# Half of wq's last rows in lanes 0 to 63, and another order of the last group's products

## The chip, the cores and the metric

The kernel runs on one core of a Trainium2 chip. The metric is the device time of one execution in microseconds, the median of three runs. The profile is of one execution of the same program, taken by the hardware profiler.

## The reference

Two branches of a decoder block act on one token of each of four batch rows, and are added to the input. x has the shape 4 x 1 x 640; all data are bfloat16.

```
xn  = layernorm(x)
q   = xn @ wq                          # 640 x 4096: 32 heads of 128
s   = q . k_cache / sqrt(128)          # k_cache: 4 x 32 x 4096 x 128
o   = softmax(s) @ v_cache             # v_cache: the same shape
z   = gelu(xn @ w_in);  z1, z2 = halves of z;  z2 = layernorm(z2)
g   = w_sp * z2 + b_sp
out = x + o @ wo + (z1 * g) @ w_out
```

Each of the two caches is 134 MB, and every element is read once.

## The kernel before, in words

**Tiles.** The caches are read in 32 tiles each. A tile is one group of four heads (hg) of one batch row (b), 4 MB: 128 lanes of 32 KB. There are eight groups of four batch rows, taken in that order. `load` (L115) issues a tile on SP's queue into one of five buffers (`slot`, L79) of 32 KB a lane. `pump` (L137) issues the next load as soon as the buffer's former occupant has been used; the order is written out in `loads` (L125 to L132): two key tiles, then value and key in turn, with two extra key tiles late in the run. The last value tile goes in four pieces, cut by V_CUTS at 64, 96 and 112 of the 128 rows that a lane holds.

**Start.** ACT issues x (L83) and two single numbers, wsp and bsp (L94, L95). SP issues wq in two transfers (L89): five rows of wq belong to each lane, four of them (4096 KB) go into one buffer and the fifth (1024 KB, 8 KB a lane) into a second one. Then SP issues w_in and w_out in three transfers into a third buffer (L100 to L104), then the first key tiles. DVE and ACT normalise x, and PE transposes it (L202) into xnT, 128 lanes by five columns of four. q comes from 40 products (L217): for each half r of the eight groups and each of the five rows c, four products write four quarters of the PSUM lanes. Then follow `stage_q` (L379), which spreads q over the lanes, and `gmlp` (L268), the second branch.

**The loop** (L569) handles key tile i and value tile j = i minus the lag. DVE multiplies the key tile with q (`product`) and halves it (`fold_half`), PE sums it (`sums`), DVE and ACT make the softmax weights (`row_sums`, `head_max`, `exps`), and PE multiplies them into the value tile (`weighted`, L462): 32 products with the weights as the stationary operand and 512 value columns moving. Two batch rows (a = 0 or 1) of a group share one PSUM tile, `pvs[hg, a]`; `take` (L481) copies it to `o_rows` with ACT. The rows of a group stand spread in it, and products with a 0/1 matrix, `pick`, gather them (`group_pick`, L498); `group_proj` (L527) multiplies with a tile of wo into the sum that is kept in PSUM.

**The end** (L596 to L643) is written out by hand. `load_wo(7)` issues the last wo tile in four pieces of 160 KB, one for each head, behind the last value tile. Then, in PE's order: value tile 30 (32 products of L471), the sums of the weights (`den`, L604), the first 64 rows of value tile 31 as 16 wide products of L471, ACT's copy (`take`), 8 products with `pick` for both a (L616, each two instructions as the data are float32), and the remaining 64 rows of tile 31 as 64 narrow products (L625) in which the values are the stationary operand and four columns of weights move. DVE divides (L633), `group_proj` makes eight products (L531), and ACT and DVE copy the result out.

Inside the block of L563 the order on PE, DVE, ACT and SP is that of the program. Ahead of it the framework orders the instructions, and it places all semaphores by itself, those of the DMAs too.

Of the kernel before, what the change touches and what calls it, by code (L numbers as in the profile page):

```python
# [9 lines left out]
FP32 = mybir.dt.float32  # L10
BF16 = mybir.dt.bfloat16
# [10 lines left out]
def kernel(  # L22
# [14 lines left out]
    nc = tc.nc  # L37
    P = nc.NUM_PARTITIONS
    Bsz, Sq, D = A_x.shape
    _, H, S, Dh = A_k_cache.shape  # L40
    HD = A_wq.shape[1]
    F = B_w_in.shape[1]
    Fh = F // 2
    DC = D // P
# [4 lines left out]
    HT = 4  # L49
    HG = H // HT  # L50
    NT = HG * Bsz
    LN = P // HT
    NC = HT * S // P
# [8 lines left out]
    QD = 32  # L62
    CB = 4
    NG = NC // CB
    GW = CB * Dh
    MC = CB * HT

    const = ctx.enter_context(tc.tile_pool(name="const", bufs=1))
# [3 lines left out]
    small = ctx.enter_context(tc.tile_pool(name="small", bufs=2))  # L72
# [3 lines left out]
    ps_m = ctx.enter_context(tc.tile_pool(name="ps_m", bufs=3, space=PSUM))  # L76
    ps_out = ctx.enter_context(tc.tile_pool(name="ps_out", bufs=1, space=PSUM))

    def slot(name):  # L79
        return kv.tile([P, SLOT], BF16, tag="kv", name=name)  # L80
# [2 lines left out]
    nc.scalar.dma_start(out=x_bf[:], in_=A_x.flatten_outer_dims())  # L83

    wq_v = A_wq.rearrange("(p c) n -> p c n", c=DC)
    wq_parts = []
    for c0, c1 in ((0, HT), (HT, DC)):
        t = slot("wq")[:, 0 : (c1 - c0) * HD].rearrange("p (c n) -> p c n", n=HD)
        nc.sync.dma_start(out=t, in_=wq_v[:, c0:c1, :])  # L89
        wq_parts += [(t, i) for i in range(c1 - c0)]  # L90

    wsp_bf = const.tile([1, 1], BF16)
    bsp_bf = const.tile([1, 1], BF16)
# [8 lines left out]
        out=w_out_sb[:, 0:NFF, :], in_=B_w_out[0 : NFF * P].rearrange("(p k) n -> p k n", k=NFF)  # L102
# [10 lines left out]
    V_CUTS = (0, 64, 96, 112, NC)  # L113
# [45 lines left out]
    ident = const.tile([P, P], BF16)  # L159
# [5 lines left out]
    ones_sq = const.tile([P, P], FP32)  # L165
    nc.vector.memset(ones_sq[:], 1.0)

    NACC = 2
    p_m = [const.tile([P, NG, QD], BF16, name=f"pm{b}") for b in range(Bsz)]
    acc = [const.tile([P, HT, QD], FP32, name=f"acc{g}") for g in range(NACC)]  # L170
# [9 lines left out]
    for i in range(NSTAT):  # L180
# [5 lines left out]
        out=rstd[:], in_=mv[:, 1:2], func=ACT.Sqrt, bias=eps_tile[:Bsz], scale=1.0  # L186
    )
    nc.vector.reciprocal(out=rstd[:], in_=rstd[:])
    xn_bf = work.tile([Bsz, D], BF16)
    nc.vector.tensor_scalar(  # L190
        out=xn_bf[:],
# [9 lines left out]
    for c in range(DC):  # L201
        nc.tensor.transpose(  # L202
            out=xnT_ps[:, c, :], in_=xn_v[:, c, :], identity=ident[:Bsz, :Bsz]
        )
    xnT = const.tile([P, DC, QD], BF16)
    nc.vector.memset(xnT[:], 0.0)
    nc.vector.tensor_copy(out=xnT[:, :, 0:Bsz], in_=xnT_ps[:])

    QB = HG // CB
    q_rows = []  # L210
    for r in range(QB):
        q_ps = ps_pv.tile([P, GW], FP32, tag="pv", name="q_ps")
        for c in range(DC):
            t, i = wq_parts[c]
            for g in range(CB):
                hg = r * CB + g
                nc.tensor.matmul(  # L217
                    out=q_ps[g * QD : (g + 1) * QD, :],
                    lhsT=xnT[:, c, :],
                    rhs=t[:, i, hg * GW : (hg + 1) * GW],  # L220
                    start=(c == 0),
                    stop=(c == DC - 1),
                )
        rows = const.tile([P, GW], BF16, name=f"q_rows{r}")
        nc.vector.tensor_copy(out=rows[:], in_=q_ps[:])  # L225
        q_rows.append(rows)
# [5 lines left out]
        out=hot[:],  # L232
        in_=ident[:].rearrange("p (g t m) -> p t m g", g=P // QD, t=2),
# [3 lines left out]
    for a in range(2):  # L237
        for t in range(2):
            nc.vector.tensor_copy(
                out=pick[:, a, :, :, 2 * a + t],  # L240
                in_=hot[:, t, :].rearrange("p (c h) -> p c h", c=CB),
# [5 lines left out]
    def out_sum(half):  # L247
        return out_ps[OG * half : OG * half + Bsz, :]

    for half in range(2):  # L250
        nc.tensor.matmul(
            out=out_sum(half),
            lhsT=ident[:Bsz, :Bsz],
            rhs=x_bf[:, half * NOH : (half + 1) * NOH],
            start=True,
            stop=False,
# [122 lines left out]
    def stage_q(i):  # L379
        hg, b = divmod(i, Bsz)  # L380
        r, g = divmod(hg, CB)
        row = g * QD + b
        qb_ps = ps_m.tile([P, HT, Dh], FP32, tag="m", name="qbc_ps")
        nc.tensor.matmul(  # L384
            out=qb_ps[:],
            lhsT=ident[:, row : row + 1].to_broadcast([P, P]),
            rhs=q_rows[r][:],
            start=True,
            stop=True,
        )  # L390
        qbcs[i] = small.tile([P, Dh], BF16, name="qbc", bufs=3)
        for hh in range(HT):
            ps = slice(hh * LN, (hh + 1) * LN)
            nc.scalar.copy(out=qbcs[i][ps, :], in_=qb_ps[ps, hh, :])  # L394
# [64 lines left out]
                accum_out=a[ps, hh, b : b + 1],  # L459
            )  # L460

    def weighted(i, c1=NC):  # L462
        hg, b = divmod(i, Bsz)
        a, t = divmod(b, 2)
        if t == 0:
            pvs[hg, a] = ps_pv.tile([P, GW], FP32, tag="pv", name="pv")
        v_nat, pm = v_tiles[i], p_m[b]
        ng = c1 // CB
        for g in range(ng):
            cg = g % CB  # L470
            nc.tensor.matmul(  # L471
                out=pvs[hg, a][cg * QD : (cg + 1) * QD, :],
                lhsT=pm[:, g, :],
                rhs=v_nat[:, g * CB : (g + 1) * CB, :],
                start=(t == 0 and g < CB),
                stop=(t == 1 and g >= ng - CB),
            )

    gr, taken = {}, {}
# [1 line left out]
    def take(hg, a):  # L481
        o = taken[hg, a] = small.tile([P, CB, Dh], FP32, name="o_rows")
        nc.scalar.copy(out=o[:].rearrange("p c d -> p (c d)"), in_=pvs.pop((hg, a))[:])  # L483
# [59 lines left out]
    def at(i, fn, *args):  # L543
        if 0 <= i < NT:
            fn(i, *args)
# [17 lines left out]
    with tc.manual_schedule(engines={E.PE, E.DVE, E.Activation, E.SP}):  # L563
        stage_q(0)
        stage_q(1)
        gmlp()
        used.update(occupants[:3])
        pump()
        for i in range(NT):  # L569
            j = turns.get(i)  # L570
            last = turns.get(i - 1, -1)
            product(i, 0)
            at(i - 1, row_sums, 1)
            at(i - 1, head_max)
            group(last, group_pick)
            fold_half(i, 0)
            at(i - 1, exps)
            sums(i, 0)
            group(last, group_turn)
            if i + 2 < NT:  # L580
                stage_q(i + 2)
            product(i, 1)
            due = [] if j is None else [j]
            if i == NT - 1:
                due += range(j + 1, NT - 2)
            for jj in due:
                consume(jj)
            row_sums(i, 0)
            fold_half(i, 1)
            sums(i, 1)  # L590
            group(last, group_proj)
            used.add(("k", i))
            pump()
            if i % Bsz == 2 and i // Bsz < HG - 1:
                load_wo(i // Bsz)
        load_wo(HG - 1)  # L596
        row_sums(NT - 1, 1)
        head_max(NT - 1)
        exps(NT - 1)
        weighted(NT - 2)  # L600

        hg, b = HG - 1, Bsz - 1
        den = ps_m.tile([P, HT, Bsz], FP32, tag="m", name="den_all")
        nc.tensor.matmul(  # L604
            out=den[:], lhsT=ones_sq[:], rhs=acc[hg % NACC][:, :, 0:Bsz], start=True, stop=True
        )
        rden = small.tile([P, HT, Bsz], FP32, name="rden_all")
        nc.vector.reciprocal(out=rden[:], in_=den[:])  # L608

        weighted(NT - 1, V_CUTS[1])  # L610
        take(hg, 1)
        o_ps = ps_m.tile([P, HT, Bsz], FP32, tag="m", name="o_last")
        for a in range(2):
            o = taken.pop((hg, a))
            for c in range(CB):
                nc.tensor.matmul(  # L616
                    out=o_ps[:],
                    lhsT=o[:, c, :],
                    rhs=pick[:, a, c, :, 0:Bsz],
                    start=(a == 0 and c == 0),  # L620
                    stop=False,
                )
        pm = p_m[b][:].rearrange("p g (t c h) -> p g t c h", t=2, c=CB)
        for c in range(V_CUTS[1], NC):
            nc.tensor.matmul(  # L625
                out=o_ps[:, :, b],
                lhsT=v_tiles[NT - 1][:, c, :],
                rhs=pm[:, c // CB, b % 2, c % CB, :],
                start=False,
                stop=(c == NC - 1),  # L630
            )
        o_n = small.tile([P, HT, Bsz], BF16, name="o_n_last")
        nc.vector.tensor_tensor(out=o_n[:], in0=o_ps[:], in1=rden[:], op=ALU.mult)  # L633
        gr[hg] = o_n
        group_proj(hg)

        res = work.tile([P, NOH], BF16, name="res")
        out_v = out.flatten_outer_dims()
        r0, r1 = slice(0, Bsz), slice(OG, OG + Bsz)
        nc.scalar.copy(out=res[r0], in_=out_ps[r0])  # L640
        nc.vector.tensor_copy(out=res[r1], in_=out_ps[r1])
        nc.scalar.dma_start(out=out_v[:, 0:NOH], in_=res[r0])
        nc.sync.dma_start(out=out_v[:, NOH:D], in_=res[r1])  # L643
# [30 lines left out]
```

## Time and profile before

| What | Value |
|---|---|
| median of three runs | 666.87 us (666.75 to 668.23) |
| the profiled execution: its own time | 668.35 us |
| the profiled execution: span from first to last instruction | 666.6 us |
| busy: PE, DVE, ACT | 46%, 75%, 19% of the span |
| bytes read, mean rate | 282.24 MB, 423 GB/s |
| rate in the first and the last of 40 slices | 373 and 243 GB/s |
| rate in the slices between | 421 to 439 GB/s |
| mean TensorE clock granted | 0.734 of full speed |

The page gives, for each engine, the busy time; the span cut into 40 slices; the DMA queues; the chain of work that ended last, followed back from the last instruction; and the costliest groups of instructions. A busy share is a mean over stages with different limits. In a timeline row stand start, duration, engine, line, operation, the tile written and the tiles read, the count, and in brackets the idle time before it with what ended it. SPq and ACTq rows are issues of DMAs: their duration is that of the issue and not of the transfer, and a row that holds two issues covers the wait between them. A tile's view gives the time from a DMA's issue to its landing.

### The profile page before, as it was taken

How to read it: one execution, taken by the hardware profiler on the slowest of the kernel's cores; microseconds unless marked ns; L12 is line 12 of the kernel's file. 1: busy time of each engine (PE TensorE's matmuls, PEld its weight loads, DVE VectorE, ACT ScalarE, POOL GpSimd, SP SyncE). 2: the span in 40 equal slices, each digit the busy share in tenths (PEclk: the TensorE clock that was granted, in tenths of full speed). 3: DMA queues.
4: the chain of work that ended last, by engine and by line, in shares of the span. 5: the costliest groups of instructions: out<-in, count | busy, mean ns of one | idle time of the engine just before them, and what ended most of it. 6: DMA issues, size and time to landing. Idle time of an engine off the chain costs nothing.

```text
span 666.6 us, 5047 instructions
## 1 busy us (share of the span) xinstructions
PE 304.9 (46%) x1985; PEld 125.7 (19%) x1985; DVE 499.6 (75%) x350; ACT 127.2 (19%) x441; POOL 4.7 (1%) x15
## 2 busy tenths in 40 slices
PE   2536443534436234553336543345453455335457
PEld 0312111211112111211113111121111212113124
DVE  2299797877788777788777688777788899776960
ACT  0302222111222111222120222120222122120130
POOL 2000000000000000000000000000000000000000
PEclk9667765888767678776678856798766777778585
DMA  9999999999999999999999999999999999999996
GB/s 373 421 435 432 421 439 432 427 433 430 427 427 432 437 435 426 433 424 429 433 436 427 430 429 433 431 432 433 424 433 435 426 431 433 426 433 435 428 421 243
DMA packets 11971, 282.57 MB, mean 424 GB/s; under 512 B 1344, under 2 KB 1964, under 8 KB 3244
## 3 DMA queue, kind: packets, MB, share of 16 engines
q1 hardware_dynamic: 11928, 282.25, 98.9%
q8 instruction: 15, 0.25, 0.1%
q14 instruction: 8, 0.07, 0.0%
q10 hardware_dynamic: 20, 0.01, 0.0%
HBM read 282.24 MB, written 0.01 MB: 423 GB/s over the span
## 4 chain that ended last, share of the span: by engine, by line
DMA 68%; DVE 23%; PE 7%; issue 2%; DVEq 0%
DMA k_nat<-in_A_k_cache_dram 62%; DVE k_nat L400 12%; DVE k_nat L409 7%; PE s_ps L418 4%; DMA v_nat<-in_A_v_cache_dram 4%; DVE s_sb L429 2%; DMA wq<-in_A_wq_dram 2%; PE pv L471 1%; PE q_ps L217 1%; PE o_last L616 1%; DVE m L438 0%; DVE mt L440 0%; DVE o_n L514 0%; DVE nm L442 0%; PE o_last L625 0%
## 5 line engine op out<-in xcount | busy, mean ns | idle before, releaser
L400 DVE TENSOR_TENSOR k_nat<-k_nat,qbc 128x8192 bf16<-128x8192 bf16 x64 | 282.7, 4418 | 106.3 <-DMA k_nat<-in_A_k_cache_dram 106.0
L418 PE MATMUL s_ps<-k_nat,ident 128*128 128x512 bf16 x512 | 181.1, 518 | 331.9 <-DVE k_nat L409 331.8
L409 DVE TENSOR_TENSOR k_nat<-k_nat 128x4096 bf16<-128x4096 bf16 x64 | 146.0, 2281 | 0.0
L418 PEld LDWEIGHTS <-ident 128*128 128x128 bf16 x512 | 62.2, 121 | 434.2 <-issue 359.2
L471 PE MATMUL pv<-v_nat,pm 128*32 128x512 bf16 x1008 | 72.9, 441 | 6.5 <-DMA v_nat<-in_A_v_cache_dram 6.5
L448 ACT ACTIVATE nb<-nm 128x1 f32<-128x1 f32 x32 | 6.5, 203 | 354.2 <-DVE nm L442 354.2
L453 ACT ACTIVATE pm<-s_sb,nb 32x128 bf16<-32x128 f32 x128 | 71.7, 560 | 2.7
L394 ACT CAST qbc<-qbc_ps 32x128 bf16<-32x128 f32 x128 | 32.9, 257 | 135.1 <-PE qbc_ps L384 134.0
L429 DVE TENSOR_REDUCE s_sb<-s_ps 128x64 f32<-128x512 f32 x64 | 43.7, 682 | 2.0 <-PE s_ps L418 2.0
L471 PEld LDWEIGHTS <-pm 128*32 128x32 bf16 x1008 | 26.9, 109 | 59.1 <-issue 44.5
L453 ACT ACTIVATION_READ_ACCUMULATOR pm<-s_sb,nb 32x1 f32 x128 | 30.1, 235 | 0.0
L384 PE MATMUL qbc_ps<-q_rows,ident 128*128 128x512 bf16 x32 | 18.0, 568 | 0.0
L503 PEld LDWEIGHTS o_ps<-o_rows,pick 128*128 128x128 f32 x112 | 15.9, 218 | 1.4 <-issue 0.6
L503 PE MATMUL o_ps<-o_rows,pick 128*128 128x128 f32 x112 | 15.6, 300 | 0.0
L483 ACT COPY o_rows<-pv 128x512 f32<-128x512 f32 x16 | 9.4, 586 | 30.3 <-PE pv L471 30.3
L495 DVE RECIPROCAL rden<-den 128x1 f32<-128x1 f32 x7 | 1.2, 168 | 14.0 <-PE den L487 14.0
L438 DVE TENSOR_REDUCE m<-s_sb 128x1 f32<-128x128 f32 x32 | 9.2, 286 | 1.1
L225 DVE CAST q_rows<-q_ps 128x512 bf16<-128x512 f32 x2 | 1.4, 692 | 11.3 <-PE q_ps L217 11.3
L217 PE MATMUL q_ps<-wq,xnT 128*32 128x512 bf16 x40 | 4.6, 605 | 7.5 <-DMA wq<-in_A_wq_dram 7.5
L440 DVE STREAM_TRANSPOSE mt<-m 128x32 f32<-128x32 f32 x32 | 6.8, 211 | 1.1
L442 DVE TENSOR_REDUCE nm<-mt 128x1 f32<-128x32 f32 x32 | 6.0, 186 | 1.1
L608 DVE RECIPROCAL rden_all<-den_all 128x16 f32<-128x16 f32 x1 | 0.3, 258 | 8.5 <-PE den_all L604 8.5
(83 smaller groups left out, 75.1 us busy)
## 6 DMA issues: line engine op xcount, KB each, us to landing
k_nat<-in_A_k_cache_dram SPq DMA_DIRECT2D x32, 4096.0 KB, 41.3
v_nat<-in_A_v_cache_dram SPq DMA_DIRECT2D x31, 4096.0 KB, 35.9
wo<-in_A_wo_dram SPq DMA_DIRECT2D x7, 640.0 KB, 42.3
wq<-in_A_wq_dram SPq DMA_DIRECT2D x1, 4096.0 KB, 13.0
w_sb<-in_B_w_in_dram SPq DMA_DIRECT2D x1, 2160.0 KB, 19.7
v_nat<-in_A_v_cache_dram SPq DMA_DIRECT2D x1, 2048.0 KB
wq<-in_A_wq_dram SPq DMA_DIRECT2D x1, 1024.0 KB, 15.0
v_nat<-in_A_v_cache_dram SPq DMA_DIRECT2D x1, 1024.0 KB
```

The source lines that it names most:

```text
L217: nc.tensor.matmul(out=q_ps[g * QD : (g + 1) * QD, :], lhsT=xnT[:, c, :], rhs=t[:, i, hg * GW : (hg + 1) * GW], start=(c == 0), stop=(c == ...
L384: nc.tensor.matmul(out=qb_ps[:], lhsT=ident[:, row : row + 1].to_broadcast([P, P]), rhs=q_rows[r][:], start=True, stop=True,)
L394: nc.scalar.copy(out=qbcs[i][ps, :], in_=qb_ps[ps, hh, :])
L400: nc.vector.tensor_tensor(out=half_of(i, half), in0=half_of(i, half), in1=qbcs[i][:, None, :].to_broadcast([P, HC, Dh]), op=ALU.mult,)
L409: nc.vector.tensor_tensor(out=t[:, :, 0:HD2], in0=t[:, :, 0:HD2], in1=t[:, :, HD2:Dh], op=ALU.add)
L418: nc.tensor.matmul(out=s[:], lhsT=ident[:], rhs=t[:, :, g * RW : (g + 1) * RW], start=(g == 0), stop=(g == n - 1),)
L429: nc.vector.tensor_reduce(out=scores[i][:, half * HC : (half + 1) * HC], in_=sums_ps.pop((i, half))[:], axis=AX.X, op=ALU.add,)
L438: nc.vector.tensor_reduce(out=m1[:], in_=scores[i][:], axis=AX.X, op=ALU.max)
L453: nc.scalar.activation(out=pm[ps, :, b % 2, :, hh], in_=s_sb[ps, :].rearrange("p (g c) -> p g c", c=CB), func=ACT.Exp, bias=nb[ps], scale= ...
L471: nc.tensor.matmul(out=pvs[hg, a][cg * QD : (cg + 1) * QD, :], lhsT=pm[:, g, :], rhs=v_nat[:, g * CB : (g + 1) * CB, :], start=(t == 0 and ...
L483: nc.scalar.copy(out=o[:].rearrange("p c d -> p (c d)"), in_=pvs.pop((hg, a))[:])
L503: nc.tensor.matmul(out=o_ps[:], lhsT=pick[:, a, c, :, :].rearrange("p h q -> p (h q)"), rhs=o[:, c, :], start=(a == 0 and c == 0), stop=(a ...
```

## The change

**wq.** The fifth row of each lane is split by columns. Its first 2048 columns go as before to all 128 lanes (`wq_wide`, 512 KB). The other 2048 columns of these 128 rows go to lanes 0 to 63, two rows in each (`wq_tall`, 512 KB), in eight transfers of eight lanes that stand four apart: lanes 0, 4, ... 28, then 1, 5, ... 29, and so on, then the same from lane 32. SP thus issues ten transfers for wq and not two. x is transposed a second time for these rows (`xhT`, 64 lanes, two columns of four). In q the groups 0 to 3 take their fifth product from `wq_wide`, and the groups 4 to 7 take two products of 64 lanes from `wq_tall`: 44 products and not 40.

**The last group.** The four 0/1 products of a = 0 (`pick_last(0)`) are issued ahead of value tile 30. `weighted(30)` closes the sum of a = 1; ACT's copy follows at once, then `den`, then `pick_last(1)`. The last value tile is no longer multiplied in part by `weighted`: all its 128 rows go through narrow products in which the values are the stationary operand.

```diff
+    wq_main = slot("wq")[:].rearrange("p (c n) -> p c n", n=HD)
+    nc.sync.dma_start(out=wq_main, in_=wq_v[:, 0:HT, :])
+    wq_rest = slot("wq")
+    wq_wide = wq_rest[:, 0:HDW]
+    nc.sync.dma_start(out=wq_wide, in_=wq_v[:, HT, 0:HDW])
+    wq_tall = wq_rest[:, HDW : 3 * HDW].rearrange("p (j n) -> p j n", j=2)
+    tall_v = A_wq.rearrange("(l j c) n -> l j c n", j=2, c=DC)
+    STEP = 4
+    for at0 in range(0, HP, QD):
+        for r in range(STEP):
+            lanes = slice(at0 + r, at0 + QD, STEP)
+            nc.sync.dma_start(out=wq_tall[lanes], in_=tall_v[lanes, :, HT, HDW:HD])
...
+    xh_v = xn_bf[:].rearrange("b (l j c) -> b j c l", j=2, c=DC)
+    for j in range(2):
+        nc.tensor.transpose(
+            out=xhT_ps[:, j, :], in_=xh_v[:, j, HT, :], identity=ident[:Bsz, :Bsz]
+        )
...
+            if r == 0:
+                yield xnT[:, HT, :], wq_wide[:, cols]
+            else:
+                cut = slice(hg * GW - HDW, (hg + 1) * GW - HDW)
+                for j in range(2):
+                    yield xhT[:, j, :], wq_tall[0:HP, j, cut]
...
-        weighted(NT - 2)
...
-        weighted(NT - 1, V_CUTS[1])
-        take(hg, 1)
...
+        pick_last(0)
+        weighted(NT - 2, closing=True)
+        take(hg, 1)
+        den = ps_m.tile([P, HT, Bsz], FP32, tag="m", name="den_all")
...
+        pick_last(1)
         pm = p_m[b][:].rearrange("p g (t c h) -> p g t c h", t=2, c=CB)
-        for c in range(V_CUTS[1], NC):
+        for c in range(NC):
             nc.tensor.matmul(
                 out=o_ps[:, :, b],
                 lhsT=v_tiles[NT - 1][:, c, :],
```

More of the change, by code (lines that the diff above doesn't have):

```diff
@@ L85 @@
     wq_v = A_wq.rearrange("(p c) n -> p c n", c=DC)
[L86 to L90, printed above, removed]
+    HDW = HD // 2
+    HP = P // 2
+    wq_main = slot("wq")[:].rearrange("p (c n) -> p c n", n=HD)
[10 more added lines that the diff above has]
+            nc.sync.dma_start(out=wq_tall[lanes], in_=tall_v[lanes, :, HT, HDW:HD])
     wsp_bf = const.tile([1, 1], BF16)
@@ L207 @@
     nc.vector.tensor_copy(out=xnT[:, :, 0:Bsz], in_=xnT_ps[:])
+    xh_v = xn_bf[:].rearrange("b (l j c) -> b j c l", j=2, c=DC)
+    xhT_ps = ps_m.tile([HP, 2, Bsz], BF16, tag="m")
+    for j in range(2):
+        nc.tensor.transpose(
+            out=xhT_ps[:, j, :], in_=xh_v[:, j, HT, :], identity=ident[:Bsz, :Bsz]
+        )
+    xhT = const.tile([HP, 2, QD], BF16)
+    nc.vector.memset(xhT[:], 0.0)
+    nc.vector.tensor_copy(out=xhT[:, :, 0:Bsz], in_=xhT_ps[:])
     QB = HG // CB
@@ L212, with terms @@
         q_ps = ps_pv.tile([P, GW], FP32, tag="pv", name="q_ps")
-        for c in range(DC):
-            t, i = wq_parts[c]
+        def terms(hg):
+            cols = slice(hg * GW, (hg + 1) * GW)
+            for c in range(HT):
+                yield xnT[:, c, :], wq_main[:, c, cols]
+            if r == 0:
[4 more added lines that the diff above has]
+                    yield xhT[:, j, :], wq_tall[0:HP, j, cut]
+        todo = [list(terms(r * CB + g)) for g in range(CB)]
+        n = len(todo[0])
+        for c in range(n):
             for g in range(CB):
-                hg = r * CB + g
                 nc.tensor.matmul(
                     out=q_ps[g * QD : (g + 1) * QD, :],
-                    lhsT=xnT[:, c, :],
-                    rhs=t[:, i, hg * GW : (hg + 1) * GW],
+                    lhsT=todo[g][c][0],
+                    rhs=todo[g][c][1],
                     start=(c == 0),
-                    stop=(c == DC - 1),
+                    stop=(c == n - 1),
                 )
@@ L460, in exps, with weighted @@
             )
-    def weighted(i, c1=NC):
+    def weighted(i, closing=False):
         hg, b = divmod(i, Bsz)
@@ L467, in weighted @@
         v_nat, pm = v_tiles[i], p_m[b]
-        ng = c1 // CB
-        for g in range(ng):
+        for g in range(NG):
             cg = g % CB
@@ L475, in weighted @@
                 start=(t == 0 and g < CB),
-                stop=(t == 1 and g >= ng - CB),
+                stop=((t == 1 or closing) and g >= NG - CB),
             )
@@ L599, with pick_last @@
         exps(NT - 1)
-        weighted(NT - 2)
         hg, b = HG - 1, Bsz - 1
[L603 to L608, printed above, removed]
-        weighted(NT - 1, V_CUTS[1])
-        take(hg, 1)
         o_ps = ps_m.tile([P, HT, Bsz], FP32, tag="m", name="o_last")
-        for a in range(2):
+        def pick_last(a):
             o = taken.pop((hg, a))
@@ L622 @@
                 )
+        pick_last(0)
+        weighted(NT - 2, closing=True)
+        take(hg, 1)
+        den = ps_m.tile([P, HT, Bsz], FP32, tag="m", name="den_all")
+        nc.tensor.matmul(
+            out=den[:], lhsT=ones_sq[:], rhs=acc[hg % NACC][:, :, 0:Bsz], start=True, stop=True
+        )
+        rden = small.tile([P, HT, Bsz], FP32, name="rden_all")
+        nc.vector.reciprocal(out=rden[:], in_=den[:])
+        pick_last(1)
         pm = p_m[b][:].rearrange("p g (t c h) -> p g t c h", t=2, c=CB)
-        for c in range(V_CUTS[1], NC):
+        for c in range(NC):
             nc.tensor.matmul(
```

## The prediction

> **What bounds the kernel now.** I read the page first, then stages of the trace, then the two ends of the run. The queue table and the chain on the page:
>
> ```profile
> q1 hardware_dynamic: 11928, 282.25, 98.9%
> ...
> DMA 68%; DVE 23%; PE 7%; issue 2%; DVEq 0%
> ```
>
> SP's queue keeps the 16 DMA engines busy for 98.9% of the span. The stage table gives a DMA share of 1.00 to 1.01 in every 50 us from 100 to 650, so time that the transfers lose at the start is not won back later. What is left to decide lies at the two ends. The stage table of the last microseconds (columns after PEclk: DMA share, GB/s):
>
> ```profile
> 657.00:658.00 1.00, 1.00 (x9) 0.90 (x5) 0.00 (x0) 0.59 (x1) 0.00 (x0) 0.50 1.01 385
> 658.00:659.00 1.00, 1.00 (x6) 1.00 (x7) 0.00 (x0) 0.00 (x0) 0.00 (x0) 0.50 0.76 294
> 659.00:660.00 1.00, 1.00 (x6) 1.00 (x6) 0.00 (x0) 0.00 (x0) 0.00 (x0) 0.50 0.64 239
> 660.00:661.00 1.00, 1.00 (x22) 1.00 (x22) 0.00 (x0) 0.00 (x0) 0.00 (x0) 0.50 0.57 196
> 661.00:662.00 1.00, 1.00 (x44) 1.00 (x41) 0.00 (x0) 0.00 (x0) 0.00 (x0) 0.50 0.12 40
> ```
>
> The share falls to about 0.6 three microseconds before the transfers end: some engines are done at 658, about nine work on to 661. Meanwhile PE is full. Its timeline there:
>
> ```profile
> 655.27 1.90 PE L471 MATMUL pv<-v_nat,pm 128*32 128x512 bf16 x16 [0.67 <-DMA v_nat<-in_A_v_cache_dram]
> ...
> 657.11 3.60 PE L616 MATMUL o_last<-pick,o_rows 128*128 128x16 f32 x16
> ...
> 660.54 1.85 PE L625 MATMUL o_last<-pm,v_nat 128*128 128x4 bf16 x64
> ...
> 662.66 1.23 PE L531 MATMUL out_ps<-wo,o_n_last 128*4 128x320 bf16 x8 [0.27 <-DVE o_n_last L633]
> ```
>
> The L531 products start when DVE's o_n_last is ready. The last quarter of wo, issued at 650.34, lands 12.0 us later by the wo tile's view, at 662.3. So PE is the later of the two by 0.36 us only. The start, by SP's timeline and its waits:
>
> ```profile
> 0.74 0.87 SPq L89 DMA_DIRECT2D wq<-in_A_wq_dram  x2
> 1.66 0.47 SPq L100 DMA_DIRECT2D w_sb<-in_B_w_in_dram  x1
> ...
> 3.61 10.44 SPq L120 DMA_DIRECT2D k_nat<-in_A_k_cache_dram  x2
> ```
> ```profile
> SPq L153 <- DMA v_nat<-in_A_v_cache_dram: 16.0, 2, 9.4
> ...
> SPq L120 <- DMA wq<-in_A_wq_dram: 9.7, 1, 9.7
> ```
>
> The second key tile has a free buffer, yet SP holds it 9.7 us until the first wq transfer has landed (13.70). In order of issue, with ACT's three small ones, the DMAs are x, wq, wsp, bsp, wq, w_in, w_out, w_out, k0, k1: the tenth waits for the second. At the end the third and fourth wo pieces wait in the same way for the value tiles eight places before them. The trace's semaphore numbers agree: there are eight, used in turn, and a DMA waits until the one eight places before it has landed.
>
> **The change, part by part.** *wq at the start.* One DMA of 1024 KB becomes one of 512 KB and eight of 64 KB; bytes are the same. The order is now x, main, wsp, bsp, wide, t0, t1, t2, t3, t4 to t7, w_in. t4 is tenth and waits for main; t7 waits for wide; w_in waits for t0. Queued behind t4 on SP are w_in, w_out and all key tiles. Until now w_in was in the queue at 1.66; it now goes out thus. Main is unchanged and lands at 13.70; t4 goes at 13.72. Unblocked issues follow each other by about 0.45 us (0.74 to 1.19, 633.12 to 633.59), so w_in goes at 13.72 + 4 x 0.45 = 15.52 (wide lands near 14.95 and t0 by 15.25, not later). What the engines have meanwhile: a 32 KB row takes 1.21 us, so wide's 32 KB per engine is gone 1.2 us after main, at 13.2 to 14.6, and an engine that gets none of the eight stands empty. Main itself shows the restart: issued at 0.74, its 262 KB per engine (8 rows, 9.68 us) are through at 12.02 at the earliest by the packet records, so it flowed from 2.34, 1.60 us after its issue. w_in would flow from 15.52 + 1.60 = 17.12 on an empty engine; before, from 14.48: 2.64 us later. Engines kept warm by t4 to t7 (8 KB, 0.31 us each) save the slow first row and are limited by the 1.0 us from issue to first packet (0.74 to 1.77): 16.5, 2.0 later. I take **+2.3**, between the two, since I cannot name the engines that end last. Bounds: SP's spacing could be 0.33 (its shortest DMA row; w_in then at 15.3) or 0.81 (its longest, w_out; w_in at 16.96, 1.44 later), so +1.8 to +4.1.
>
> Moving 256 KB from lanes 64 to 127 to lanes 0 to 63 is 32 KB per engine, 1.21 us either way. That counts only if the queue never runs dry; after a dry spell both halves start w_in together, so I put its gain at 0.
>
> *q on PE and DVE.* Two transposes, a memset and a copy fall into PE's wait of 7.5 us before main; four more products of L217 (0.11 us each, from 40 in 4.55) delay q by 0.45. Under cover: key tile 0 lands at 34.7, q's rows are done at 19. Uncovered it would be 0.5 to 1.
>
> *The last group.* Half the 0/1 products (8 of the 16 instructions of L616, 0.225 us each) move into PE's idle time between 644.7 and 650.4. After tile 30 (3.60 from 650.46, so 654.06) come the copy (ACT, 0.59), beside it the sum matmul of L604 (0.61), then the other eight (1.8): 656.55. The 16 wide products of L471 go (1.90) and 64 narrow ones of L625 are added (1.85 for 64). PE then follows the pieces of tile 31: 64 narrow to 658.4; piece two is there (658.0); piece three lands at 659.3; piece four, issued at 632.64, 27.9 later at 660.55, so 661.0; L633 and its hand-over 0.25: ready at 661.3 instead of 662.66. Now **wo is late next**. Its quarters land at 660.99, 661.44, 661.88 and 662.30 by the trace's landing records; six of eight L531 products run as they come, the last two start at 662.34 and take 0.58: 662.92, where before L531 ended at 663.92. Gain **1.0**; copy and output after it are as before. If L531 had to wait for all of wo it would be 0.36, the other bound (the value pieces are waited for one by one, so I take 1.0).
>
> **Sum** against the profiled execution (span 666.6 in 668.35, so 1.75 around it): +2.3 - 1.0 = +1.3, 669.65. The median shown, 666.87, lies 1.48 under that execution; the same +1.3 gives **668.2**. About 0.3%, 2.0 us, is what a measurement here can tell from no change (the three runs span 1.48).
>
> **Rivals.** (1) *Slower, by the dry queue at the start, in full.* SP spends on each small DMA what it spent on w_out (0.81 against 0.45). Then w_in goes at 16.96 and the delay is 2.0 + 1.44 = 3.4 to 4.1; less 1.0, +2.4 to +3.1: up to **669.9**. It decides once w_in is issued after about 16.2. For: the w_out row, and transfers on only some engines are new to SP here. Against: most issue rows are 0.33 to 0.47.
> (2) *No wait.* If t4 need not wait, the transfers flow on, and the balance decides. If the late engines serve lanes 64 to 127, wo lands 0.8 to 1.2 earlier: -1.8 to -2.2, **664.9**; if they serve lanes 0 to 63, +1.2 - 1.0, 667.1. Against: ten DMAs ahead of w_in on SP and eight semaphores; wherever ACT's small ones stand, one of t4 to t6 meets main's.
> (3) *It does not do what it says*: the eight spread over all 16 engines. Then no byte changes sides, all engines stay warm, the delay is 2.0: 2.0 - 1.0, **667.9**. For: nothing in this trace shows eight lanes. Against: x, four lanes, moved as four packets of 1280 B. [...]
>
> **Chances.** Forecast 0.62: restart +1.5 to +3.0, tail -1.0, so 667.4 to 668.9, nearly all within 0.3%. Rival 1: 0.22, most of it over 2.0. Rival 2: 0.10, half of it faster by over 2.0. Rival 3: 0.06, same. With 0.06 of the forecast lying over 2.0 and 0.02 for the scatter of the medians: faster 0.05, same 0.67, slower 0.28. The range leaves out rival 2 and a little above: 666.6 to 670.0.
>
> **What would show it.** Right: SP's timeline has a gap before the fifth small wq DMA up to about 13.7, w_in issued near 15.5, a DMA share well under 1 between 13.5 and 17, gMLP's L276 starting about 2.3 later than 21.38; in the tail L531 waits for wo, and the DMA still ends unevenly. Wrong: no gap, w_in issued before 8 us (rival 2); issue rows near 0.8 (rival 1); an L531 that still waits for o_n_last; DMA ends together.

## The result, and the profile after

The changed kernel takes **669.81 us** (median of 6 runs, 669.65 to 670.47), the kernel before 667.0 in the runs beside it (6 runs, 666.75 to 668.23): a ratio of 1.0037 [1.0027, 1.0048]. 2.8 us are lost, somewhat more than the 2.0 that count as a difference. The profiled execution took 669.85, with a span of 668.1.

The queue and chain rows of the page after, to be held against those of before:

```profile
q1 hardware_dynamic: 12120, 282.25, 98.8%
...
DMA 68%; DVE 23%; PE 6%; issue 2%; SPq 1%; DVEq 0%
```

The bytes are the same, in 192 packets more. New is SPq in the chain: an issue now stands on the path that ends last. SP's timeline at the start, and its waits:

```profile
1.19 0.41 SPq L92 DMA_DIRECT2D wq<-in_A_wq_dram  x1
1.65 14.98 SPq L99 DMA_DIRECT2D wq<-in_A_wq_dram  x8
16.67 0.44 SPq L109 DMA_DIRECT2D w_sb<-in_B_w_in_dram  x1
...
18.09 1.94 SPq L129 DMA_DIRECT2D k_nat<-in_A_k_cache_dram  x2
```
```profile
SPq L99 <- DMA wq<-in_A_wq_dram: 9.2, 1, 9.2
```

L99 are the eight small transfers. Four go out at once; the fifth is held 9.2 us until the main part of wq has landed, and goes at 13.82 by the trace's single records. w_in, which before was in the queue at 1.66, follows at 16.67. What the engines do meanwhile, in the stage table (the last two columns: DMA share, GB/s):

```profile
13.00:14.00 1.00, 0.15 (x4) 0.13 (x7) 0.00 (x0) 0.00 (x0) 0.00 (x0) 1.00 0.81 328
14.00:15.00 1.00, 1.00 (x12) 0.36 (x8) 0.00 (x0) 0.00 (x0) 0.00 (x0) 1.00 0.45 180
15.00:16.00 1.00, 1.00 (x16) 0.42 (x12) 0.00 (x0) 0.00 (x0) 0.00 (x0) 1.00 0.24 70
16.00:17.00 1.00, 1.00 (x16) 0.47 (x12) 0.69 (x1) 0.00 (x0) 0.00 (x0) 1.00 0.41 115
17.00:18.00 1.00, 1.00 (x13) 0.12 (x2) 0.00 (x0) 0.04 (x1) 0.00 (x0) 1.00 1.03 229
18.00:19.00 1.00, 0.14 (x1) 0.00 (x0) 0.00 (x0) 0.97 (x4) 0.00 (x0) 1.00 0.52 146
```

Before, the same table gives 1.01 and 430 GB/s on average over 13 to 20 us; two of its rows:

```profile
15.00:16.00 1.00, 1.00 (x13) 0.46 (x6) 0.00 (x0) 0.00 (x0) 0.00 (x0) 1.00 1.03 439
16.00:17.00 1.00, 1.00 (x13) 0.38 (x11) 0.05 (x1) 0.00 (x0) 0.00 (x0) 1.00 0.93 397
```

From 14 to 17 the engines now move 70 to 180 GB/s, and even at 17 to 19, with w_in issued, only 146 to 229. By the packet records, the first engine is through with w_in at 23.67, where it was at 19.60: **+4.07**. gMLP's products start at 25.5 and not at 21.4. The tail, in PE's timeline:

```profile
657.67 1.89 PE L636 MATMUL o_last<-pick,o_rows 128*128 128x16 f32 x8 [0.15 <-ACT o_rows L513]
659.40 3.24 PE L656 MATMUL o_last<-pm,v_nat 128*128 128x4 bf16 x112
663.29 0.59 PE L656 MATMUL o_last<-pm,v_nat 128*128 128x4 bf16 x16 [0.65 <-DMA v_nat<-in_A_v_cache_dram]
664.14 1.25 PE L561 MATMUL out_ps<-wo,o_n_last 128*4 128x320 bf16 x8 [0.27 <-DVE o_n_last L664]
```

Half the 0/1 products are gone from this stretch (1.89 us and not 3.60), and PE waits for the last value piece: the brackets of the third row name a DMA. The brackets of the last row speak of the first of its eight products only. The last two start at 664.96, and the last quarter of wo lands at 664.92 by the landing records: these two wait for wo, as predicted. They end 0.93 after the last quarter of wo is through at the engines (665.39 and 664.46); before it was 2.12 (663.89 and 661.77). The end of the transfers is as uneven as before:

```profile
661.00:662.00 1.00, 1.00 (x42) 1.00 (x38) 0.00 (x0) 0.00 (x0) 0.00 (x0) 0.50 0.90 347
...
663.00:664.00 1.00, 0.59 (x16) 0.50 (x16) 0.09 (x1) 0.00 (x0) 0.00 (x0) 0.50 0.66 234
664.00:665.00 1.00, 0.86 (x8) 0.46 (x8) 0.09 (x1) 0.00 (x0) 0.00 (x0) 0.50 0.16 58
```

Between the two profiled executions, then, the end of the transfers moved by 664.46 - 661.77 = +2.7 and the stretch behind it by 0.93 - 2.12 = -1.2, together +1.5, which is 669.85 - 668.35. The medians differ by 2.8. The missing 1.3 belongs to the kernel before: its executions have **two times**, about 666.9 and about 668.2, with none between 667.4 and 667.9 in 75 runs (34 of them are of the lower). The execution that was profiled is one of the upper, the median of the runs shown one of the lower.

### The profile page after: what moved, and what is told of

Read it like the earlier page. It is cut to its first block, busy times and chain, and to the rows that moved or that the text cites. A ratio compares the mean times of both kernels' runs of the same rounds, so it can differ in the third digit from the quotient of the medians.

```text
span 668.1 us, 5169 instructions
## 1 busy us (share of the span) xinstructions
PE 306.5 (46%) x2039; PEld 129.5 (19%) x2039; DVE 499.7 (75%) x352; ACT 127.0 (19%) x441; POOL 4.7 (1%) x15
## 2 busy tenths in 40 slices
DMA packets 12164, 282.58 MB, mean 423 GB/s; under 512 B 1408, under 2 KB 2028, under 8 KB 3564
## 4 chain that ended last, share of the span: by engine, by line
DMA 68%; DVE 23%; PE 6%; issue 2%; SPq 1%; DVEq 0%
DMA k_nat<-in_A_k_cache_dram 62%; DVE k_nat L431 12%; DVE k_nat L440 7%; PE s_ps L449 5%; DMA v_nat<-in_A_v_cache_dram 4%; DMA wq<-in_A_wq_dram 2%; DVE s_sb L460 2%; PE pv L501 1%; SPq L129 1%; DVE m L469 0%; SPq L99 0%; DVE mt L471 0%; DVE o_n L544 0%; DVE nm L473 0%; PE out_ps L561 0%
## 5 line engine op out<-in xcount | busy, mean ns | idle before, releaser
L501 PE MATMUL pv<-v_nat,pm 128*32 128x512 bf16 x992 | 69.0, 428 | 4.9 <-DMA v_nat<-in_A_v_cache_dram 4.9
L533 PEld LDWEIGHTS o_ps<-o_rows,pick 128*128 128x128 f32 x112 | 19.5, 261 | 2.1 <-issue 1.4
L533 PE MATMUL o_ps<-o_rows,pick 128*128 128x128 f32 x112 | 18.8, 340 | 0.0
```

Source lines behind the costliest of these rows:

```text
L501: nc.tensor.matmul(out=pvs[hg, a][cg * QD : (cg + 1) * QD, :], lhsT=pm[:, g, :], rhs=v_nat[:, g * CB : (g + 1) * CB, :], start=(t == 0 and ...
L533: nc.tensor.matmul(out=o_ps[:], lhsT=pick[:, a, c, :, :].rearrange("p h q -> p (h q)"), rhs=o[:, c, :], start=(a == 0 and c == 0), stop=(a ...
```

## The experiments

**The theory:** the transfers lose their time at the start, because the tenth DMA in order of issue waits for the second, and w_in, w_out and the key tiles stand behind it on SP. **The rivals:** the bytes that were moved to other lanes (on other engines, or slower to take); and the tail, worse and not better.

**The two halves of the change by themselves.** The kernel before with the wq part alone:

```diff
+    STEP = 4
+    for at0 in range(0, HP, QD):
+        for r in range(STEP):
+            lanes = slice(at0 + r, at0 + QD, STEP)
+            nc.sync.dma_start(out=wq_tall[lanes], in_=tall_v[lanes, :, HT, HDW:HD])
...
         weighted(NT - 2)
...
         weighted(NT - 1, V_CUTS[1])
```

> The ten wq transfers of the change alone, with the last group as before. Theory (the dry queue): SP stands at the fifth small transfer until the main wq transfer has landed near 13.8, and issues w_in at 16.7; the first key tile lands about 4 later than before, and the whole run ends 3 to 4 us later than before, because the tail no longer gives 1.0 back. Rival (the narrow products of the last tile are what costs): no change against before. Rival (the bytes moved to lanes 0 to 63 make these engines late): +1.2 at most, and w_in issued early.

Measured: 670.2 us (6 runs, 669.5 to 671.39), ratio 1.0041 [1.0029, 1.0053]. With w_in issued at 16.60 the whole loss is here. Its profiled tail held a surprise. PE's clock (the figure ahead of the last two) and the old run of sixteen 0/1 products:

```profile
655.00:660.00 5.00, 3.77 (x44) 1.98 (x37) 0.26 (x1) 0.57 (x1) 0.00 (x0) 0.87 0.99 405
```
```profile
659.32 1.96 PE L647 MATMUL o_last<-pick,o_rows 128*128 128x16 f32 x16
```

The same sixteen instructions that took 3.60 before, at a clock of 0.50, take 1.96 at 0.87, and the old order ends with the old L531 products (here L562) starting at 664.19, as early as the new order's in the change (664.14). So in this profile the old tail costs nothing; what it costs in the profile of before comes with the clock at 0.50.

The tail alone:

```diff
+        pick_last(0)
+        weighted(NT - 2, closing=True)
+        take(hg, 1)
...
+        pick_last(1)
...
-        for c in range(V_CUTS[1], NC):
+        for c in range(NC):
```

> The new order of the last group alone, with wq as before. Theory: the last eight products of the projection wait for the quarters of wo and no longer for the division; they end about 0.6 after the last quarter has landed instead of 1.6, so the run is 1.0 us faster than before. Rival (the narrow products cost more than the wide ones): slower than before, up to the 2.8 of the whole change.

Measured: **666.8 us** (11 runs, 666.52 to 667.02), ratio 0.9987 [0.9978, 0.9995]. That is less than both kernels take. It has a single time, 0.1 below the lower one of before and 1.4 below the upper. Its PE timeline:

```profile
660.09 0.59 PE L625 MATMUL o_last<-pm,v_nat 128*128 128x4 bf16 x16 [0.69 <-DMA v_nat<-in_A_v_cache_dram]
660.95 1.32 PE L530 MATMUL out_ps<-wo,o_n_last 128*4 128x320 bf16 x8 [0.27 <-DVE o_n_last L633]
```

PE waits for the last value piece and then needs 2.2 us more, at a clock of 0.50 in this stretch: nothing that PE is slow at lies ahead of that piece any more. The rival that the tail is worse falls, and the wq part costs 669.81 - 666.8 = 3.0 on top of the new tail.

**The wait, taken away: two misses.** Two ACT loads fewer ahead of the small ones should let fewer of them meet the wait:

```diff
-    nc.scalar.dma_start(out=wsp_bf[:], in_=B_w_sp[0:1, 0:1])
-    nc.scalar.dma_start(out=bsp_bf[:], in_=B_b_sp[0:1].rearrange("(a b) -> a b", a=1))
...
     with tc.manual_schedule(engines={E.PE, E.DVE, E.Activation, E.SP}):
+        nc.scalar.dma_start(out=wsp_bf[:], in_=B_w_sp[0:1, 0:1])
+        nc.scalar.dma_start(out=bsp_bf[:], in_=B_b_sp[0:1].rearrange("(a b) -> a b", a=1))
```

> The change with the two single numbers wsp and bsp issued by ACT later, so that the sixteenth of the start's semaphore turns falls elsewhere: by the rule of the eighth place the seventh small wq transfer waits for the main one and not the fifth. Two issues of 0.71 fewer stand behind the wait. Theory: w_in is issued near 15.3 instead of 16.67 and the run is about 1.4 us faster than the change, 1.4 slower than before. Rival (bytes or lanes are the cost, not the wait): the same time as the change, 2.8 slower than before.

Measured: 669.8 us (5 runs, 669.63 to 670.15), ratio 1.0034 [1.0022, 1.0046]. The trace shows why nothing changed: ACT has nothing ahead of these two and still issues them at 1.33 and 1.58. The fifth small one waited as before, w_in went at 16.36. It repeats the change and says nothing of the theory.

Four transfers of 128 KB in place of eight, in lanes 0 to 31, four rows each:

```diff
+    NR = 4
+    HP = P // NR
+    wq_tall = wq_rest[:, HDW : (1 + NR) * HDW].rearrange("p (j n) -> p j n", j=NR)
...
+    for r in range(STEP):
+        lanes = slice(r, HP, STEP)
+        nc.sync.dma_start(out=wq_tall[lanes], in_=tall_v[lanes, :, HT, HDW:HD])
```

> The change with the same bytes in lanes 0 to 31 (four rows in each) by four transfers of 128 KB instead of eight of 64 KB, and wsp and bsp later: the same eight engines get the same extra bytes, but w_in is the eighth transfer in order and waits for none. Theory: w_in is issued before 6 us, the queue never runs dry, and the tail's 1.0 remains. If the engines of lanes 64 to 127 are the ones that end late, another 0.8 to 1.2 comes on top: 1.8 to 2.2 faster than before. If those of lanes 0 to 31 end late, about 0.2 slower than before. Rival (the small transfers themselves are slow, whatever waits): slower than before by 2 or more.

Measured: 669.1 us (12 runs, 668.11 to 670.0), ratio 1.002 [1.0012, 1.0028]. Here w_in itself is the tenth, since wsp and bsp again went early: held to 13.47, 3.2 earlier than in the change. The first engine is through with it at 20.8. A smaller delay, a smaller loss, but the run without a wait that it was meant to be it is not. (Its twelve times lie far apart, and the profile is of one of the slowest, 669.98.)

**No wait, the same bytes in the same lanes.** The last kernel with wsp and bsp on GpSimd's queue, so that w_in is eighth of those that SP and ACT issue:

```diff
+    nc.gpsimd.dma_start(out=wsp_bf[:], in_=B_w_sp[0:1, 0:1])
+    nc.gpsimd.dma_start(out=bsp_bf[:], in_=B_b_sp[0:1].rearrange("(a b) -> a b", a=1))
```

> The same extra bytes in lanes 0 to 31 by four transfers of eight lanes and 128 KB, with wsp and bsp issued by GpSimd, whose transfers take their turns apart: now w_in is the eighth in order on SP and ACT and need not wait. Theory: w_in is issued before 6 us, no dry stretch, and what is left is the shift of 1.2 us of work from eight engines to the other eight. If the engines of lanes 64 to 127 end late by themselves, the last quarter of wo lands 0.8 to 1.2 earlier than with the tail alone (666.8): 665.6 to 666.0. If not, it lands up to 1.2 later: 667.5 to 668.0. Rival (small transfers are slow in themselves): near 669.8 as the change.

```profile
1.63 3.23 SPq L99 DMA_DIRECT2D wq<-in_A_wq_dram  x4
4.90 0.44 SPq L109 DMA_DIRECT2D w_sb<-in_B_w_in_dram  x1
...
13.38 0.34 SPq L113 DMA_DIRECT2D w_sb<-in_B_w_out_dram  x1
```

Measured: 668.57 us (11 runs, 668.3 to 668.94), ratio 1.0011 [1.0002, 1.002]. w_in goes at 4.90 and the tenth, now the second w_out, is the one that is held (13.38). GpSimd's two have semaphores of their own in this trace, so they take no turn among the eight of SP and ACT. No dry spell is left (DMA share 0.93 or more in each microsecond from 13 to 22), and yet it is 1.8 slower than the tail alone. (This run and the next three were timed on another chip than the tail alone; the kernel before has its two times on both, 0.1 higher here, so that much can be the chip's.) The bytes show why: eight engines are through with w_in at 18.53 to 19.37, the other eight at 21.0 to 21.4 (all at 19.6 to 20.6 in the tail alone). The eight-lane transfers do go to eight engines only, and what those get more is still missing at the end. The stage table at the end, of this run and then of the tail alone:

```profile
660.00:661.00 1.00, 0.59 (x16) 0.50 (x16) 0.00 (x0) 0.00 (x0) 0.00 (x0) 0.50 0.37 123
661.00:662.00 1.00, 0.48 (x16) 0.48 (x16) 0.00 (x0) 0.00 (x0) 0.00 (x0) 0.50 0.27 93
662.00:663.00 1.00, 0.73 (x11) 0.40 (x8) 0.17 (x1) 0.00 (x0) 0.00 (x0) 0.50 0.12 40
```
```profile
660.00:661.00 1.00, 0.64 (x18) 0.56 (x19) 0.18 (x1) 0.00 (x0) 0.00 (x0) 0.50 0.54 186
661.00:662.00 1.00, 1.00 (x8) 0.45 (x8) 0.00 (x0) 0.00 (x0) 0.00 (x0) 0.50 0.05 17
```

A longer and thinner end: the slowest engine is 5.43 behind the first (3.47 in the tail alone), the last quarter of wo is through at 662.70 and not at 661.34. When the queue does not run dry, the shift thus costs about 1.4 at wo and 1.8 in the time. So the eight engines that got fewer bytes were not the only late ones, as the shift would need to gain anything. A share of 0.27 of sixteen engines is about four, and not eight, while 0.54 in the tail alone is about nine. That fits late engines on both sides; no run here tells them apart.

**The same lanes from all 16 engines.** Sixteen lanes in each transfer, two rows each, in lanes 0 to 63:

```diff
+    HP = P // 2
+    wq_tall = wq_rest[:, HDW : 3 * HDW].rearrange("p (j n) -> p j n", j=2)
...
     for r in range(STEP):
         lanes = slice(r, HP, STEP)
```

> As the run with four transfers and no wait, but each of the four takes sixteen lanes (four apart, lanes 0 to 63, two rows each), so that all sixteen engines carry it and no engine has more bytes than another. Theory: w_in early, no dry stretch, no shift: the time of the tail alone, 666.8. If it is the lanes written and not the engines that carry them which decide, it goes the way of the run with eight lanes.

Measured: 668.55 us (11 runs, 668.07 to 668.97), ratio 1.001 [1.0001, 1.0018]. w_in waits for nothing (issued at 4.50; the tenth, again the second w_out, goes at 13.74), and no engine gets more bytes than another. The loss is in the rate. The stage table:

```profile
14.00:15.00 1.00, 1.00 (x13) 0.36 (x8) 0.00 (x0) 0.00 (x0) 0.00 (x0) 1.00 1.14 238
15.00:16.00 1.00, 0.68 (x12) 0.16 (x5) 0.00 (x0) 0.00 (x0) 0.00 (x0) 1.00 1.46 331
```

The engines count as busy (1.14 and 1.46), yet move 238 and 331 GB/s; in the tail alone the same slices have 1.19 and 504, 1.11 and 475. By the packet records, the 4 KB packets of these transfers soon follow each other after 0.30 to 0.33 us on each engine, where those of `wq_wide` just ahead of them took 0.16. w_in is through 1.5 later on all engines. In the run before, eight engines sent such packets at 0.16 each. Eight at 0.16 or sixteen at 0.32 give the same: about 206 GB/s (an estimate from these times), where 32 KB packets of 1.215 us on sixteen engines give 431. So these packets flowed at about half that rate in both runs, from eight engines into lanes 0 to 31 and from sixteen into lanes 0 to 63. Why sixteen engines were no faster than eight, no run here shows.

**Fewer transfers behind the wait.** The change, with wsp and bsp on GpSimd's queue; the seventh small one is the tenth DMA:

```diff
-    nc.scalar.dma_start(out=wsp_bf[:], in_=B_w_sp[0:1, 0:1])
-    nc.scalar.dma_start(out=bsp_bf[:], in_=B_b_sp[0:1].rearrange("(a b) -> a b", a=1))
+    nc.gpsimd.dma_start(out=wsp_bf[:], in_=B_w_sp[0:1, 0:1])
+    nc.gpsimd.dma_start(out=bsp_bf[:], in_=B_b_sp[0:1].rearrange("(a b) -> a b", a=1))
```

> The change with wsp and bsp issued by GpSimd: by the rule of the eighth place the seventh small transfer waits for the main one, not the fifth. Two issues of 0.71 fewer stand between the wait's end and w_in. Theory: w_in issued near 15.1 instead of 16.4 to 16.7, and the run 1.2 to 1.4 faster than the change: 668.5. Rival (the bytes of lanes 0 to 63 are the cost): as the change, 669.8.

Measured: 668.98 us (11 runs, 668.66 to 670.75), ratio 1.0019 [1.001, 1.0028]. w_in goes at 15.42, 1.25 earlier than in the change; the time is 0.8 shorter. (The profile that has the 15.42 is of the slowest of these runs, 670.75.) The direction is right, the size below what was expected: part of what is gained at the start is not found at the end.

**The wait alone.** The tail alone, and eight loads of two bytes ahead of w_in; what they load is used by nothing:

```diff
+    tiny = const.tile([1, 8], BF16)
+    for n in range(8):
+        nc.sync.dma_start(out=tiny[:, n : n + 1], in_=A_wq[n : n + 1, 0:1])
```

> The tail alone with wq as before in two transfers, and eight loads of a single number each, which nothing uses, issued by SP between wq and w_in: turns of the semaphores are used up and no bytes are moved between lanes. Theory: the fifth of them waits for main, the eighth for the rest of wq (landed at 16.2), so w_in is issued near 16.5, flows near 18.4 instead of 14.5, and the run ends about 3 later than with the tail alone: 669.8. Rival (lanes or bytes are the cost): as the tail alone, 666.8.

Its SP timeline and stage table:

```profile
1.65 14.62 SPq L99 DMA_DIRECT2D tiny<-in_A_wq_dram  x8
16.31 0.36 SPq L104 DMA_DIRECT2D w_sb<-in_B_w_in_dram  x1
```
```profile
14.00:15.00 1.00, 1.00 (x16) 0.52 (x12) 0.00 (x0) 0.00 (x0) 0.00 (x0) 1.00 0.69 287
15.00:16.00 1.00, 1.00 (x13) 0.32 (x5) 0.00 (x0) 0.00 (x0) 0.00 (x0) 1.00 0.04 16
16.00:17.00 1.00, 1.00 (x13) 0.57 (x15) 0.18 (x1) 0.00 (x0) 0.00 (x0) 1.00 0.00 0
```

Measured: 669.48 us (9 runs, 669.17 to 669.82), ratio 1.0026 [1.0016, 1.0035]. No byte of wq changes its lane or engine, nothing but sixteen bytes is added, and 2.7 of the change's 3.0 us are lost. The engines stand still for nearly two microseconds, before w_in's issue and after it. This shows the theory: the place in the order of issue makes the loss, and the moved bytes are not needed for it. The two losses do not add up: 2.7 for the wait alone and 1.8 for the bytes alone would be 4.5, and the change loses 3.0.

**The two times of before.** If they come from PE's clock, and if the clock stays up while PE is busy (a guess of the author's that this run was to try), keeping PE busy in its gap ahead of value tile 30 should leave the lower one. 24 products whose result is used by nothing:

```diff
+        warm = ps_m.tile([P, GW], FP32, tag="m", name="warm")
+        for _ in range(24):
+            nc.tensor.matmul(
+                out=warm[:], lhsT=ident[:], rhs=q_rows[0][:], start=True, stop=True
+            )
```

> The kernel before, with 24 products of 128x512 that nothing uses, put on PE between the sums of the last key tile and value tile 30, where PE waits nearly 6 us for data. Theory: the kernel before has two times, near 666.9 and near 668.1, because its tail hangs on PE and PE's granted clock in the tail is sometimes full and sometimes 0.5; with PE kept busy the 0/1 products take about 2 us instead of 3.6, and all runs come out near 666.8, the time of the tail alone. So most of what the new order of the last group brings is that the end no longer depends on PE's clock. Rival (the two times come from the transfers): two times as before, or slower by the added products.

Measured: 667.33 us (11 runs, 666.81 to 668.37; before 667.0), ratio 0.9999 [0.999, 1.0008]. Three of its eleven runs are still at the upper time. The profiled one is among them, and shows where the edit fell short:

```profile
650.62 1.91 PE L471 MATMUL pv<-v_nat,pm 128*32 128x512 bf16 x32
...
655.02 1.90 PE L471 MATMUL pv<-v_nat,pm 128*32 128x512 bf16 x16 [2.16 <-DMA v_nat<-in_A_v_cache_dram]
656.85 3.60 PE L621 MATMUL o_last<-pick,o_rows 128*128 128x16 f32 x16
```

Tile 30's products now take 1.91 and not 3.60 (clock 0.99 from 650 to 655, before 0.50), so PE is done early, waits 2.16 for the next piece, and the 0/1 products run slow as ever (3.60, clock 0.50 from 655 to 660). So this run does not settle whether the clock makes the two times.

The kernel before, unchanged, was profiled once more in the hope of the lower time:

> The kernel before, unchanged, for another profile. If it falls on the lower of its two times (about 666.9), PE's granted clock should be near 1.0 in the last ten microseconds, the 0/1 products should take about 2 us instead of 3.6, and the projection should wait for wo. If it falls on the upper one, the profile is as the one shown.

Measured: 668.31, the upper time again, with the clock at 0.50 and 3.60 for the 0/1 products. That the lower time of before is a tail with the clock up is therefore shown only beside it: by the wq part's own profile, which has the same tail at 0.87, and by the tail alone, which has no upper time. For before itself no profile shows it. The runs give one number more: over a whole execution, the granted clock is 0.731 on average in the 30 lower executions for which it is listed, and 0.723 in the 39 upper ones. Ten microseconds at half clock in 666 would make 0.0075 (an estimate), and the difference is 0.008. That agrees with the clock as the cause, but a mean over the run does not say where in it the clock was lower.

## Why the prediction was right, and where it was wrong

**The mechanism: right.** The gap before the fifth small transfer, up to 13.82 (13.72 predicted), w_in behind it, a DMA share under 1 from 13 to 17, gMLP later, the last two products waiting for wo, an uneven end: all as written. The wait for wo is short: the first three pairs of these products start 0.22 and 0.27 apart, and the last pair 0.33 behind the third. Rival 2 (no wait) is refuted by the 9.2 us of L99.

**SP's price for a small transfer: mis-sized.** The prediction took 0.45 us from one issue to the next, from the plain transfers. Measured: 16.67 - 13.82 = 2.85 for four, 0.71 each, and a row of 0.67 each in L99's own view. It lay within the bounds (0.33 to 0.81), nearer to the row that I had set aside (w_out's 0.81). w_in was issued 1.15 later than predicted, 1.05 of it for this and 0.10 since the main part landed later. This is rival 1's condition, w_in after 16.2, and its 669.9 is nearest to the median.

**The restart: mis-sized.** Predicted 1.0 to 1.6 us from issue to flow. w_in's bytes take an engine 5.1 us (14.49 to 19.61 in the tail alone), so in the change it is as if they had flowed from 23.67 - 5.1 = 18.55, 1.9 after the issue. The eight tiny loads give 1.7, the two behind the wait 1.8. The records show both parts of it: the first packet starts 1.15 after the issue, and the first packets take 0.8 to 1.6 us and not 0.65. Keeping half the engines busy in the change did not shorten it (1.9, against 1.7 with the tiny loads). The term came out at +4.07, against +2.3 predicted, at the upper bound of 4.1.

**"Time that the transfers lose at the start is not won back": not quite.** Against the tail alone, +4.06 at w_in is +3.12 at the last quarter of wo and +3.0 in the time. The eight tiny loads had +3.53 at w_in, +2.74 at wo and +2.7 in the time. About 0.8 to 1.0 is given back in between; by the packet records about half a microsecond of it between the 80th and the 200th of the 282 MB. The engines are no faster after a dry spell: a 32 KB packet takes 1.215 us in the change and 1.216 in the tail alone. Where it comes from stays open.

**The balance, put at 0: right here.** The eight tiny loads, with no bytes shifted, lose 2.7 of 3.0; little is left for the shift. Without a wait it costs 1.8, as the four transfers show, on the side of rival 2 that gave 667.1 and not 664.9. That an engine serves one half of the lanes, as rival 2 has it, the runs do not show: the transfers of sixteen lanes among 0 to 63 gave no engine more bytes than another.

**Rival 3: refuted.** The page after counts 1408 packets under 512 B, before 1344. By the packet records the new ones have 4 bytes, and a transfer to all lanes has sixteen of them. Sixty-four more for eight transfers is eight each: eight engines, not sixteen, and the four transfers without a wait show the two groups apart (w_in through at 18.53 to 19.37, and at 21.0 to 21.4).

**q under cover: right.** The last products of q run at 19.3 to 19.9, with PE idle behind them for 5.65 us until w_in is there. q's rows are done at 20.6 and not at 19.0, 1.6 later where 0.45 was predicted, since the last small transfers landed late.

**The tail: right in the profile, wrong in the median.** Predicted -1.0, measured -1.2 between the profiled executions. The step that failed is "the same +1.3 gives 668.2": it took what the tail saves against an execution whose PE ran at half clock, and subtracted it from a median in which that time is mostly not spent. Before's median, 1.48 below its own profiled execution, held the hint. Against the lower time the tail is worth 0.1, and the change is the start's +3.0 almost bare. Between the profiled executions the sum was +1.3 predicted, +1.5 measured; but its two terms were each off, +2.7 (after what was given back) for +2.3, and -1.2 for -1.0. The median is 1.6 above the 668.2 and above the forecast's own band, 667.4 to 668.9; that the stated range holds it is owed to the room that rival 1 was given.

## What to carry to other kernels

Count the DMAs ahead of a large load, on every queue that shares its semaphores (here SP's and ACT's): in this case a split into many small ones held a load that nothing else held, up to 16.67 us, and sixteen bytes in eight pieces cost nearly as much as the real change (2.7 of 3.0 us). Where a median lies clearly below the profiled execution, find out which term of the profile the other executions do not pay before that term is carried over. Split the parts of a change: the half that looked small here is the one to keep.

## What the runs showed of the hardware

- An issue on SP of eight lanes with two rows mostly took 0.67 us in the change (0.71 from one to the next), of whole 128-lane tiles mostly 0.33 to 0.47; the two of two bytes on ACT took 0.23 and 0.27.
- After the dry spell of the change the first packet of w_in started 1.15 us after its issue, and w_in ended as if it had flowed from 1.9 us after it (1.7 with the eight tiny loads, 1.8 with two transfers behind the wait).
- From sixteen engines into lanes 0 to 63, a 4 KB packet took 0.30 to 0.33 us, where one of `wq_wide` just ahead took 0.16: about 206 GB/s (an estimate from these times), as from eight engines at 0.16.
- The same 16 products took 3.60 us at a clock of 0.50 (before) and 1.96 at 0.87 (the wq part alone). A wait of 2.16 us ahead of them lay before the slow ones in one profile (the 24 added products).
